# Which half of a block's old keys and queries comes from the chunk that ends last

## The chip, the cores and the metric

The kernel runs on one core of one Trainium2 chip. The metric is the device time of one execution in microseconds (us). The core has five engines with a queue each: TensorE (PE; its weight loads are listed as PEld), VectorE (DVE), ScalarE (ACT), GpSimd (POOL) and SyncE (SP), which here issues DMAs only.

## The reference

Four layers run in turn over 2048 tokens of width 512: attention with a recurrent memory (A), a gated MLP (B), A, B. A's core, cut to what matters:

```python
for s in range(n_seg):                        # 64 segments of 32 tokens
    xs = x[:, s * 32:(s + 1) * 32, :]
    h = concatenate([mem, xs], axis=1)        # 8 memory rows, then 32 tokens
    q, k, v = (einsum('btd,dhe->bhte', h, W) for W in (Wq, Wk, Wv))   # 32 heads of 128
    scores = where(mask, einsum('bhqe,bhke->bhqk', q, k) * scale, -1e9)
    o = einsum('bhqk,bhke->bhqe', softmax(scores), v)
    o = einsum('bhte,hed->btd', o, Wo)
    mem = o[:, :8, :]                         # goes into the next segment
    outs.append(o[:, 8:, :])
```

Each segment needs the memory that the one before it puts out, so the 64 segments of a pass run one after the other.

## The kernel before

There are two passes over A, each 64 segments in 16 blocks of four (128 tokens), and a B layer behind each. One segment takes about 9.7 us.

**New and old rows.** A segment has 40 rows: 8 memory rows and 32 tokens. Only 32 rows fit a column group of TensorE, so the kernel multiplies 32 of them (the memory and the first 24 tokens) by Wq, Wk and Wv inside the segment. The last 8 tokens of a segment depend on no memory. They are called the *old* rows, and are projected ahead, for the four segments of a block at once: four times 8 rows are again 32 (`hB`, copied from the block's transposed input `hT` by GpSimd, L637).

**Chunks.** The projection of `hB` is cut in six chunks of 512 columns, numbered j: 0 and 1 are the queries, 2 and 3 the keys, 4 and 5 the values, the even one for *half 0* of the heads and the odd one for *half 1*. A chunk is 16 matmuls (`b_mms`, L714) into a PSUM bank. ScalarE copies it to `rowsB` (L763), and `b_out` then has it turned, so that heads lie along the free dimension: by a DMA transpose issued by SP (L768), or, for one marked `turned`, by VectorE (L766). The turned queries go to `QTB`, the keys to `KTB`, each with two halves and two buffers, by the block's parity. In the profile they have the names `front` (even blocks) and `old` (odd blocks).

**Where the chunks run.** A segment calls `fill()` three times, at places where TensorE has to wait for the other engines: ahead of `pv(0)`, ahead of the second inverse, and behind `tok_out(0)`. Each call runs the next piece of a generator. For blocks 2, 3 and 4 of the first pass and 1 to 4 of the second it is `b_even`, run over the four segments of the block before. It spreads twelve pieces: one chunk in four quarters into one PSUM bank (`accA`), two whole chunks between them in another (`accB`), and this twice. In the last of the four segments the last two quarters of the second such chunk are run and then its DMA transpose is issued; then comes the last whole chunk, which VectorE turns. Later blocks use `b_units` and are done a segment earlier.

**What a segment needs of them.** `prep_segment(s + 1)` stands at the end of segment s. GpSimd copies the 8 old rows of the segment from `QTB` into columns 32 to 39 of `QQ` (L905, both halves by one instruction of 128x256), and from `KTB` into `KX` (L909, one instruction for each half). `QQ` and `KX` have two buffers each, by the segment's parity. GpSimd's and SP's instructions are put in order by a scheduler; those of TensorE, VectorE and ScalarE stay as written.

**The scores.** `scores(r)` for half r has 16 matmuls of all 40 queries with the new keys `KA` (L975, moving operand `QQ`) and 4 of the queries with the old keys (L979, weights `KX[r]`). TensorE runs: the four projections, the start of the values of half 0, `scores(0)`, the rest of the values of half 0, half of the values of half 1, `scores(1)`. ScalarE takes the exponential (L984), and VectorE multiplies it by the mask into `E` (L987); both inputs are in SBUF. VectorE's order after `scores(0)` is: turn `KA` of half 1 (L952), `E` of half 0, `VA` of half 0 (L1073), `E` of half 1. `pv(0)` (L1024) needs `E` and `VA` of half 0.

Of the kernel before, what the change touches and what calls it, by code (L numbers as in the profile page):

```python
# [16 lines left out]
KT = 4  # L17
# [564 lines left out]
def qk_rhs(w, j, kt, cg):  # L582
    return w[j // 2][:, kt, :].rearrange("p (r gs i eb el) -> p r eb i gs el", r=2, gs=4, i=4, eb=4)[:, j % 2, cg]


def cols_rhs(w, j, kt, cg):
    at = 2048 * (j % 2) + 512 * cg
    return w[j // 2][:, kt, at:at + 512]
# [81 lines left out]
def a_block(tc, c, rows, front, MV_in, RS_in, MV_out, RS_out, ahead, wo, S, first):  # L670
# [6 lines left out]
    with ExitStack() as ctx:  # L677
# [34 lines left out]
        def mm_chunk(ps, lhs, rhs, kts=range(KT)):  # L712

            return [nc.tensor.matmul(ps[32 * cg:32 * cg + 32, :], lhsT=lhs(kt, cg), rhs=rhs(kt, cg), start=(kt == 0), stop=(kt == KT - 1),  # L714
                                     tile_position=(0, 32 * cg)) for kt in kts for cg in range(4)]
# [8 lines left out]
        NKQ = 2  # L724
        KAr = [pers.tile([P, 2, 8, 32, 2], BF16, name=f"KA{i}") for i in range(2)]
        QQr = [pers.tile([P, 2, 8, 40, 2], BF16, name=f"QQ{i}") for i in range(NKQ)]
        KXr = [[pers.tile([P, 4, 32], BF16, name=f"KX{i}{r}") for r in range(2)] for i in range(NKQ)]
        uT = [pers.tile([P, H, 32], BF16, name=f"uT{i}") for i in range(2)]
# [8 lines left out]
        def store_v(bs):  # L737
            nc.sync.dma_start(rows.vb_d[:], bs["VB"].rearrange("p i r e -> p (i r e)"))
# [8 lines left out]
        copies, turns, adds = [], [], []  # L747
# [5 lines left out]
        def b_out(bs, slot, j, ps, turned, stored):  # L753

            if j >= 4:
                nc.scalar.copy(bs["VB"][:, :, j - 4, :], ps.rearrange("p (i e) -> p i e", i=4))
                if turned:
                    ahead.regroup(bs["VB"], bs["VX"], (j - 4,))
                elif stored:
                    store_v(bs)  # L760
                return
            r = rowsB[:, slot, :]
            nc.scalar.copy(r, ps)  # L763
            t = bs[("QTB", "KTB")[j // 2]][:, j % 2]
            if turned:
                turns.append(lambda: nc.vector.transpose(out=t.rearrange("p a b -> p (a b)"), in_=r))  # L766
            else:
                nc.sync.dma_start_transpose(out=t.rearrange("p (i g) k -> p i (g k)", g=4), in_=r.rearrange("t (i e) -> t i e", i=4))  # L768

        def b_mms(bs, j, ps, kts, turned=False):  # L770
            mm_chunk(ps, lambda kt, cg: bs["hB"][:, kt, :],
                     lambda kt, cg: qk_rhs(w, j, kt, cg) if j < 4 and turned else cols_rhs(w, j, kt, cg), kts)
# [23 lines left out]
        def b_even(tb):  # L796

            bs = blk_state[tb]
            for j, others in ((4, (5, 0)), (2, (1, 3))):
                psA = accA.tile([P, 512], F32, name="psb")[:]  # L800
                for kt, other in zip((0, 2), others):
                    b_mms(bs, j, psA, (kt,))
                    yield
                    b_mms(bs, j, psA, (kt + 1,))
                    if kt == 2:
                        copies.append(lambda j=j, psA=psA: b_out(bs, 0, j, psA, False, True))
                    yield
                    psB = accB.tile([P, 512], F32, name="psb")[:]
                    b_mms(bs, other, psB, range(KT), other == 3)
                    copies.insert(0, lambda other=other, psB=psB: b_out(bs, 1, other, psB, other == 3, False))  # L810
                    yield

        def wo_pairs(px, lhs):
# [87 lines left out]
        def prep_segment(s, eng=nc.gpsimd):  # L901
            tb, j4 = s // 4, s % 4
            bs = blk_state[tb]
            QQ = QQr[s % NKQ]
            eng.tensor_copy(QQ[:].rearrange("p r n q two -> p (r n) two q")[:, :, :, 32:40],  # L905
                            bs["QTB"].rearrange("p r (n two) k -> p (r n) two k", two=2)[:, :, :, 8 * j4:8 * j4 + 8])
            KX = KXr[s % NKQ]
            for r in range(2):
                eng.tensor_copy(KX[r][:].rearrange("p g (k i) -> p i g k", i=4),  # L909
                                      bs["KTB"][:, r].rearrange("p (i g) k -> p i g k", i=4)[:, :, :, 8 * j4:8 * j4 + 8])  # L910
            seg_state[s] = dict(QQ=QQ, KX=KX, VX=bs["VX"])

        def fold(px, cross, t1, beside):
# [18 lines left out]
        def segment(s, fill, spare1, spare2, spare3, tail, loads):  # L932
            tb, j4 = s // 4, s % 4
            st = seg_state.pop(s)
            QQ, KX, VX = st["QQ"], st["KX"], st["VX"]
            KA = KAr[s % 2]
# [14 lines left out]
            def qk_T(j, r):  # L951
                nc.vector.transpose(out=(QQ[:, j % 2, :, 0:32] if j < 2 else KA[:, j % 2]).bitcast(F32).rearrange("p n q one -> p n (q one)"), in_=r[:].bitcast(F32))  # L952

# [3 lines left out]
            def ends(q):  # L957

                return q.rearrange("p h (b e) -> p h b e", e=8)[:, :, 0:5:4, :]

            def own(q):

                return q.rearrange("p (i b e) -> p i b e", i=4, b=2)
# [4 lines left out]
            def scores(r):  # L968
# [3 lines left out]
                for i in range(4):  # L972
                    for g in range(4):
                        n = 4 * i + g
                        mms.append(nc.tensor.matmul(pS[32 * g:32 * g + 32, 40 * i:40 * i + 40], lhsT=KA[:, r, n // 2, :, n % 2], rhs=QQ[:, r, n // 2, :, n % 2],  # L975
                                                    start=(i == 0), stop=True, tile_position=(0, 32 * g), skip_group_check=True))
                for g in range(4):
                    q = QQ[:, r].rearrange("p (i g) q two -> p i g two q", i=4)[:, :, g // 2, g % 2, :]
                    mms.append(nc.tensor.matmul(own(pS[32 * g:32 * g + 32, 160:224]), lhsT=KX[r][:, g, :], rhs=ends(q),  # L979
                                                start=False, stop=True, tile_position=(0, 32 * g), skip_group_check=True))  # L980
# [162 lines left out]
            if s + 1 < NSEG:  # L1143
                prep_segment(s + 1)
# [14 lines left out]
        start = nc.vector if first else nc.gpsimd  # L1159
        rows.begin(start)  # L1160
        prep_segment(0, start)
        due, ys = [], []
        seen = pers.tile([P, 1], BF16, name="seen")
# [16 lines left out]
        for s in range(NSEG):  # L1180
            tb, j4 = s // 4, s % 4
# [149 lines left out]
```

## Time and profile before

| | |
|---|---|
| timed runs, median of 3 | 1624.22 us (1623.9 to 1627.45) |
| profiled execution | 1621.89 us |
| its span on the core | 1620.2 us |
| TensorE busy | 1577.7 us, 97% of the span |
| GpSimd busy | 288.2 us, 18% of the span |
| GpSimd's copies into KX (L909) | 254, 0.54 us each in the mean |
| GpSimd's copies into QQ (L905) | 127, 0.49 us each in the mean |
| mean granted clock of TensorE | 0.998 |

The profile is of one execution, on the chip, by the hardware profiler. A row of the timeline has the start in us from the span's start, the duration, the engine, the line, the operation, what it writes and reads with shapes, the number of like instructions merged in the row and, in brackets, the idle time of the engine before it and what ended that. A row of waits has the engine and line that waited, whom for, the total, how many times, and the longest.

### The profile page before, as it was taken

How to read it: one execution, taken by the hardware profiler on the slowest of the kernel's cores; microseconds unless marked ns; L12 is line 12 of the kernel's file. 1: busy time of each engine (PE TensorE's matmuls, PEld its weight loads, DVE VectorE, ACT ScalarE, POOL GpSimd, SP SyncE). 2: the span in 40 equal slices, each digit the busy share in tenths (PEclk: the TensorE clock that was granted, in tenths of full speed). 3: DMA queues.
4: the chain of work that ended last, by engine and by line, in shares of the span. 5: the costliest groups of instructions: out<-in, count | busy, mean ns of one | idle time of the engine just before them, and what ended most of it. 6: DMA issues, size and time to landing. Idle time of an engine off the chain costs nothing.

```text
span 1620.2 us, 91261 instructions
## 1 busy us (share of the span) xinstructions
PE 1577.7 (97%) x41182; PEld 983.8 (61%) x41182; DVE 1070.7 (66%) x3059; ACT 1050.1 (65%) x2281; POOL 288.2 (18%) x604
## 2 busy tenths in 40 slices
PE   5899999999999999999999999999999999999999
PEld 2566666666666666566656656666666666665565
DVE  4576766667776776784366666666677667768622
ACT  3677777777777777660047777777777777776400
POOL 6111111112211221320011111111121112214000
PEclk9999999999999999999999999999999999999999
DMA  9412111113321333277952122121233223425696
GB/s 364 94 42 41 41 44 43 43 43 83 74 56 44 89 83 78 92 184 157 203 161 47 46 42 50 46 47 47 72 87 77 47 69 99 99 52 172 144 197 160
DMA packets 259805, 148.11 MB, mean 91 GB/s; under 512 B 193752, under 2 KB 235840, under 8 KB 259416
## 3 DMA queue, kind: packets, MB, share of 16 engines
q1 hardware_dynamic: 246184, 98.46, 27.8%
q0 software_dynamic: 13232, 43.82, 8.3%
q8 instruction: 322, 5.28, 1.4%
q14 instruction: 67, 0.55, 0.1%
HBM read 59.68 MB, written 37.19 MB: 60 GB/s over the span
## 4 chain that ended last, share of the span: by engine, by line
PE 50%; DMA 4%; DVE 2%; issue 0%; SPq 0%; ACT 0%; POOL 0%; DVEq 0%; ACTq 0%
PE psK L714 6%; PE psQ L714 6%; PE pg L397 5%; PE psb L714 5%; PE pz L296 5%; PE psO L825 4%; PE px L818 3%; PE psV L714 3%; PE psm L714 3%; PE pwB L837 2%; PE psO L1024 2%; PE psT L1016 1%; PE py L440 1%; DMA y_x<-xd 1%; DMA ln_x<-xd 1%; PE psS L975 1%
## 5 line engine op out<-in xcount | busy, mean ns | idle before, releaser
L714 PEld LDWEIGHTS <-hT 128*32 128x32 bf16 x12288 | 343.8, 97 | 265.3 <-DVE hT L924 14.0
L714 PE MATMUL psV<-Wv_sb,hT 128*32 128x512 bf16 x2048 | 165.7, 379 | 0.0
L952 DVE STREAM_TRANSPOSE QQ<-rows 128x256 f32<-128x256 f32 x256 | 113.1, 442 | 77.8 <-ACT rows L949 75.8
L949 ACT CAST rows<-psQ 128x512 bf16<-128x512 f32 x256 | 144.2, 592 | 27.6 <-PE psQ L714 24.9
L984 ACT ACTIVATE S<-psS 128x224 bf16<-128x224 f32 x256 | 92.2, 360 | 100.7 <-PE psS L979 100.5
L1045 DVE TENSOR_TENSOR uT<-psO,Rm 128x128 bf16<-128x128 f32 x256 | 74.7, 292 | 123.0 <-ACT Rm L1042 122.0
L397 PE MATMUL pg<-z,wspT 128*128 128x344 bf16 x1024 | 154.3, 309 | 0.0
L1048 DVE TENSOR_TENSOR uT<-psO,Rt 128x384 bf16<-128x384 f32 x256 | 140.4, 548 | 19.2 <-ACT Rt L1124 17.0
L952 DVE STREAM_TRANSPOSE KA<-rows 128x256 f32<-128x256 f32 x256 | 113.6, 444 | 59.5 <-ACT rows L949 56.4
L714 PE MATMUL psK<-Wv_sb,hT 128*32 128x512 bf16 x2048 | 152.0, 378 | 0.0
L1124 ACT ACTIVATE Rt<-Rt 128x512 f32<-128x512 f32 x256 | 147.3, 622 | 4.0
L825 PE MATMUL psO<-Wo_high,uT 128*32 128x128 bf16 x8192 | 140.2, 219 | 3.8 <-issue 3.7
L714 PE MATMUL psQ<-Wq_sb,hT 128*32 128x512 bf16 x2048 | 136.0, 381 | 7.1 <-DVE xo L448 2.5
L714 PE MATMUL psQ<-Wk_sb,hT 128*32 128x512 bf16 x2048 | 135.3, 380 | 0.0
L714 PE MATMUL psK<-Wk_sb,hT 128*32 128x512 bf16 x2048 | 134.8, 379 | 0.0
L714 PE MATMUL psm<-Wq_sb,hT 128*32 128x512 bf16 x2048 | 134.8, 379 | 0.0
L818 PE MATMUL px<-Wo,uT 128*32 128x256 bf16 x3840 | 133.2, 273 | 0.4
L1121 ACT ACTIVATE Rt<-psT 128x1024 f32<-128x1024 f32 x128 | 131.2, 1025 | 3.2
L397 PEld LDWEIGHTS <-wspT 128*128 128x128 bf16 x1024 | 100.2, 98 | 53.2
L825 PEld LDWEIGHTS <-uT 128*32 128x32 bf16 x8192 | 125.9, 97 | 10.4 <-issue 5.4
L818 PEld LDWEIGHTS <-uT 128*32 128x32 bf16 x4096 | 107.0, 97 | 27.0 <-DVE uT L1045 1.3
L909 POOL COPY KX<-old 128x128 bf16<-128x128 bf16 x128 | 66.0, 535 | 312.1 <-PE psS L979 194.9
(200 smaller groups left out, 2864.7 us busy)
## 6 DMA issues: line engine op xcount, KB each, us to landing
o_d<-o_sb SPq DMA_DIRECT2D x126, 64.0 KB
vb_d<-front SPq DMA_DIRECT2D x30, 256.0 KB
VX<-vb_d SPq DMA_DIRECT2D x120, 64.0 KB
ln_x<-xd SPq DMA_DIRECT2D x26, 256.0 KB
y_o<-o_d POOLq DMA_DIRECT2D x22, 256.0 KB, 3.5
xd<-y_o POOLq DMA_DIRECT2D x22, 256.0 KB, 2.9
Wq_sb<-in_A_Wq_dram POOLq DMA_DIRECT2D x8, 512.0 KB, 8.2
Wk_sb<-in_A_Wk_dram POOLq DMA_DIRECT2D x8, 512.0 KB, 10.0
```

The costliest lines, as they stand in the source:

```text
L296: nc.tensor.matmul(pz[:, c0:c1], lhsT=xnT[:, kt, :], rhs=w_in_sb[:, kt, c0:c1], start=(kt == 0), stop=(kt == KT - 1))
L397: nc.tensor.matmul(pg[t][:, k, 0:344], lhsT=wsp[t][:, st, :], rhs=z(st, 344 * k, 344 * k + 344), start=(st == 0), stop=(st == NT - 1))
L714: return [nc.tensor.matmul(ps[32 * cg:32 * cg + 32, :], lhsT=lhs(kt, cg), rhs=rhs(kt, cg), start=(kt == 0), stop=(kt == KT - 1), tile_posi ...
L818: nc.tensor.matmul(px[at:at + 32, 0:256], lhsT=lhs[:, h, :], rhs=wo_rhs(h, slice(k + 2, None, -2) if h % 2 else slice(k, None, 2)), start= ...
L825: nc.tensor.matmul(pw[32 * cg:32 * cg + 32, :], lhsT=lhs[:, h, :], rhs=wo_rhs(h, cg), start=False, stop=(h == H - 1), tile_position=(0, 32 ...
L949: return r, mms, copy(r[:].rearrange("p (n el two) -> p n el two", n=8, two=2), ps.rearrange("p (n two el) -> p n el two", n=8, two=2))
L952: nc.vector.transpose(out=(QQ[:, j % 2, :, 0:32] if j < 2 else KA[:, j % 2]).bitcast(F32).rearrange("p n q one -> p n (q one)"), in_=r[:]. ...
L984: return nc.scalar.activation(out=S[:, r], in_=psS[:, r, 0:224], func=ACT.Exp, scale=scale)
L1045: nc.vector.tensor_tensor(out=hview(uT_cur[:], r, 24, 32), in0=oview(r, 0, 8), in1=Rm[:, r].rearrange("p g (n q) -> p g n q", q=8), op=ALU ...
L1048: nc.vector.tensor_tensor(out=hview(uT_nxt[:], r, 0, 24), in0=oview(r, 8, 32), in1=rview(r, 0, 24), op=ALU.mult)
L1121: nc.scalar.activation(out=Rt[:], in_=psT[:], func=ACT.Ln)
L1124: nc.scalar.activation(out=rt, in_=rt, func=ACT.Exp, scale=-1.0)
```

## The change

In `b_even` the second quartered chunk is now 3 (half 1's keys), with the whole chunks 2 (half 0's keys) and 1 (half 1's queries) between its quarters. The last whole chunk, the one that VectorE turns, is 1. Before, the quartered one was 2, the whole ones 1 and 3, and VectorE turned 3. In `prep_segment` the copy of the old queries is cut in two instructions, one for each half, and each half's queries stand ahead of its keys. All lines behind move up by one: L975 is L974, L979 is L978 and so on; the copies into QQ are L906 and those into KX L908.

```diff
         def b_even(tb):
...
-            for j, others in ((4, (5, 0)), (2, (1, 3))):
+            for j, others in ((4, (5, 0)), (3, (2, 1))):
...
-                    b_mms(bs, other, psB, range(KT), other == 3)
-                    copies.insert(0, lambda other=other, psB=psB: b_out(bs, 1, other, psB, other == 3, False))
+                    b_mms(bs, other, psB, range(KT), other == 1)
+                    copies.insert(0, lambda other=other, psB=psB: b_out(bs, 1, other, psB, other == 1, False))
...
         def prep_segment(s, eng=nc.gpsimd):
             tb, j4 = s // 4, s % 4
             bs = blk_state[tb]
-            QQ = QQr[s % NKQ]
-            eng.tensor_copy(QQ[:].rearrange("p r n q two -> p (r n) two q")[:, :, :, 32:40],
-                            bs["QTB"].rearrange("p r (n two) k -> p (r n) two k", two=2)[:, :, :, 8 * j4:8 * j4 + 8])
-            KX = KXr[s % NKQ]
+            QQ, KX = QQr[s % NKQ], KXr[s % NKQ]
             for r in range(2):
+                eng.tensor_copy(QQ[:, r].rearrange("p n q two -> p n two q")[:, :, :, 32:40],
+                                bs["QTB"][:, r].rearrange("p (n two) k -> p n two k", two=2)[:, :, :, 8 * j4:8 * j4 + 8])
                 eng.tensor_copy(KX[r][:].rearrange("p g (k i) -> p i g k", i=4),
-                                      bs["KTB"][:, r].rearrange("p (i g) k -> p i g k", i=4)[:, :, :, 8 * j4:8 * j4 + 8])
+                                bs["KTB"][:, r].rearrange("p (i g) k -> p i g k", i=4)[:, :, :, 8 * j4:8 * j4 + 8])
             seg_state[s] = dict(QQ=QQ, KX=KX, VX=bs["VX"])
```

## The prediction, made before the changed kernel was run

> **What bounds the kernel now.** I read the page's busy table first, then the waits of TensorE (weight loads and matmuls), then the timeline at each place where those waits lie.
>
> ```profile
> PE 1577.7 (97%) x41182; PEld 983.8 (61%) x41182; DVE 1070.7 (66%) x3059; ACT 1050.1 (65%) x2281; POOL 288.2 (18%) x604
> ...
> PEclk9999999999999999999999999999999999999999
> ```
>
> TensorE is busy for 97% of the span at the full granted clock, so time can only be won where it stands still. The change touches no matmul's size or number, so only its waits matter. The waits of the weight loads and of the matmuls (engine, line, waited for: us, times, longest):
>
> ```profile
> PEld L975 <- DVE KA L952: 36.6, 144, 1.3
> PEld L979 <- POOL KX L909: 5.3, 5, 1.7
> PE psS L979 <- POOL KX L909: 4.7, 5, 1.6
> ```
>
> The last two rows are one stall, seen on both queues: five times the scores of old keys (L979) wait for GpSimd's copy of them, 4.7 us of matmul time. That is all that GpSimd's copies cost TensorE. The places are the starts of blocks 2, 3, 4 of each pass and of block 1 of the second, the seven blocks fed by `b_even`; two of the seven do not stall. The timeline of one that does (start, duration):
>
> ```profile
> 198.76 1.19 SPq L768 DMA_TRANSPOSE front<-rowsB  x1
> 199.22 0.29 POOL L637 COPY hB<-hT 128x128 bf16<-128x128 bf16 x1 [4.68 <-DMA hT<-ln_xn]
> 200.10 0.70 DVE L766 STREAM_TRANSPOSE front<-rowsB 128x512 bf16<-128x512 bf16 x1
> 202.03 0.28 PE L975 MATMUL psS<-QQ,KA 128*32 128x40 bf16 x16
> 202.66 0.45 DVE L952 STREAM_TRANSPOSE KA<-rows 128x256 f32<-128x256 f32 x1 [0.42 <-ACT rows L949]
> 203.12 1.63 POOL L909 COPY KX<-front 128x128 bf16<-128x128 bf16 x5 [3.61 <-DMA front<-rowsB]
> 203.64 0.10 PEld L979 LDWEIGHTS <-KX 128*32 128x32 bf16 x4 [1.45 <-POOL KX L909]
> 204.55 0.38 PEld L975 LDWEIGHTS <-KA 128*32 128x32 bf16 x16
> ```
>
> The quartered chunk 2 (half 0's old keys) is turned by a DMA issued at 198.76; it lands at about 203.12, when GpSimd starts its copies. Half 0's scores need the first copy and go on at 203.64, 0.52 after it. Half 1's scores begin at 204.55. VectorE turned the other late chunk at 200.10 to 200.80, long before. A boundary without a stall shows the floor for half 1's scores:
>
> ```profile
> 162.86 1.65 POOL L909 COPY KX<-old 128x128 bf16<-128x128 bf16 x5 [2.81 <-DMA old<-rowsB]
> ...
> 163.41 0.12 PEld L979 LDWEIGHTS <-KX 128*32 128x32 bf16 x4
> ...
> 163.96 0.45 DVE L952 STREAM_TRANSPOSE KA<-rows 128x256 f32<-128x256 f32 x1 [0.42 <-ACT rows L949]
> ...
> 164.46 0.25 PEld L975 LDWEIGHTS <-KA 128*32 128x32 bf16 x16 [0.23 <-DVE KA L952]
> ```
>
> They can begin 0.50 after VectorE starts turning half 1's new keys (KA), whatever GpSimd does.
>
> **The change part by part.** Chunks: matmuls, ScalarE copies, DMA turns and VectorE turns keep their number, size and place in each queue; chunks 2, 1, 3 only change slots (one matmul of Wq or of Wk takes 379 ns in either). Cost 0. What moves is who needs the late DMA: now half 0's scores, afterwards half 1's, about 1.1 us later in TensorE's order (203.64 to 204.55 plus the 0.2 of L979 itself). The turns also gain a wait for GpSimd's reads of the same buffer two blocks earlier, long over: 0.
>
> GpSimd's queue: the built program's order at such a boundary is now: queries of segments s and s+1, hB, then (late) keys half 0 of s and s+1, keys half 1 of s and s+1. Afterwards: queries and keys of half 0 for s and s+1, hB, then keys half 1 of s (these wait for the DMA), keys half 1 of s+1, queries half 1 of s, queries half 1 of s+1. So half 0 no longer stalls, but **half 1's scores now wait for the third copy behind the landing**, since their moving operand is QQ. Everything turns on this: the stall is not removed, it is moved and shortened.
>
> Let L be the start of the first late copy. Now, where there is a stall, half 1's scores begin at L+1.42 (204.55-203.12=1.43; the other four give 1.42). Afterwards: five copies take 1.63 to 1.65 with 0.47 for the last, a pitch of 0.29, so the queries' copy starts at L+0.58. Its duration, 128 elements with a stride of two, is in no row: between 0.29 (hB, 128 elements) and 0.48 (the whole 256 elements of QQ); I take 0.40, between them. Then 0.05 until TensorE moves (0.52-0.47). L+1.03. Bounds: 0.58+0.29+0.05=0.92 and 0.58+0.48+0.05=1.11, plus 0.23 if a VectorE mask product runs beside it (a KX copy that took 0.47 alone took 0.70 there): 1.34. The five stalled boundaries by L, KA's start and the present start: 124.11, 124.12, 125.53; 203.12, 202.66, 204.55; 875.43, 875.71, 876.85; 914.62, 915.17, 916.04; 955.14, 954.41, 956.56. The new start is the later of L+1.03 and KA+0.50: gains 0.39, 0.40, 0.39, 0.37, 0.39, together **1.94 us** (0.41 with 1.34, 2.38 with 0.92). The two others (L+1.03 = 163.89 and 995.91 against floors of 164.46 and 996.34) gain and lose nothing. Behind that point TensorE's queue is as before, so the gain stays.
>
> The split copies: one more GpSimd instruction in each of 128 segments. No wait in TensorE's lists but the five names GpSimd in an ordinary segment; the copies there are made for two segments ahead. What they could reach is VectorE. With half 0's queries copied ahead of its keys, GpSimd is busy 0.3 to 0.5 longer just when VectorE forms half 0's mask product E and then VA, which TensorE needs at L1024:
>
> ```profile
> 75.64 0.48 POOL L909 COPY KX<-old 128x128 bf16<-128x128 bf16 x1 [7.39 <-PE psS L979]
> 76.15 0.35 DVE L987 TENSOR_TENSOR E<-S,maskN 128x448 bf16<-128x448 bf16 x1
> 76.42 0.68 DVE L1073 CAST VA<-psK 128x512 bf16<-128x512 f32 x1
> 77.16 0.32 PE L1024 MATMUL psO<-E,VA 64*128 64x80 bf16 x8
> ```
>
> Here VA's end (77.10) is followed by L1024 after 0.06: it is the last to come. That holds in segments 1 to 3 of the first pass alone, which have no fill. Elsewhere the distance is about 0.27 (VA ends 306.74, L1024 at 307.00), so 0.21 us is cover. A single copy beside E lengthens it by 0.04 at most (0.39 at 56.78) or not at all (0.35 at 305.79, with a copy running from 305.52 to 306.00). Cost: 3 x 0.04 = 0.1; bounds 0 and 3 x 0.15 (E took 0.50 beside the train of five). If the cover were gone, see the second rival.
>
> The page "SBUF — State Buffer" of the Trainium skill, section "Who interferes with whom", speaks against the change: a VectorE instruction with two SBUF inputs and a GpSimd instruction that reads SBUF exclude each other, the later one being fully blocked. By it E would wait out the longer pair of copies in every segment. The 0.35 at 305.79 beside a running copy does not show this; the 0.70 of a copy begun just after E agrees with it.
>
> VectorE makes the first segment's copies (29.50 to 30.37); its next work is at 32.21, after 1.84 idle: 0.
>
> Sum: -1.94+0.1 = -1.8. The profiled execution took 1621.89 (span 1620.2 and 1.7 around it) and becomes 1620.1; the median of the timed runs is 2.3 above it, so 1624.2 becomes **1622.4**, 0.11% less. This kernel can be told from no change at about 0.2%, 3.2 us.
>
> **Rivals.** *The stall goes altogether* (faster). If the copies behind the late landing are in time everywhere, the gain is the present starts minus the floors: 0.91+1.39+0.64+0.37+1.65 = 4.96, so 1619.3. It needs earlier landings, not a faster copy. For it: at the two worst boundaries the hT transpose ahead on SP's queue took 2.04 and 2.23 us to issue (195.99 and 947.87) against 1.20 at 869.24, 908.63 and 989.03; with 1.0 less at these two, 0.52+0.25+0.26 of stall would remain, a gain of 3.9 and 1620.3. Against it: nothing in the change shortens that issue.
>
> *GpSimd's pair delays VectorE in every segment* (slower). If E waited for the end of both copies, it would start at 75.64+0.29+0.48 = 76.41 in place of 76.15, 0.26 late; past the cover of 0.21 that is 0.05 in each of some 121 segments, 6.0, and 0.26 in each of three, 0.8: +6.8-1.9 = +4.9, 1629.1. It decides from about 0.25 late on (each 0.01 past the cover is 1.2 us). For it: E took 0.50 for 0.35 beside the train of five (at 204.30). The page named above would lead one to expect it. Against it: even there it lost 0.15, less than the cover.
>
> *The stall only changes place* (no gain: the copies interleave with VectorE's work and L+1.34 holds): 0.4 less, 1623.8. That the change does not do what it says is excluded by the built order, except in this sense.
>
> **How the numbers follow.** The forecast with its bounds, from 2.4 less to no change, and the no-gain case: 0.74, all within 0.2%. Stall gone or nearly: 0.17, faster by over 0.2%. VectorE delayed: 0.09, slower. The range goes from 1619.3, the stall gone, to 1626.0, which takes in a small part of the VectorE case on top of the forecast; the forecast's own range is 1621.8 to 1624.3.
>
> **What would show it.** Right: L979 no longer waits for KX; instead L975's second group waits for QQ at four or five boundaries, L+1.03 after the first late copy, 3.0 us in all; the half copy of QQ takes 0.3 to 0.5; E keeps 0.35 to 0.39 in ordinary segments. Wrong: L975 waits nowhere for GpSimd (first rival), or E starts late in ordinary segments and L1024 follows VA by 0.06 (second), or a new wait on GpSimd inside blocks.

## The result, and the profile after

The changed kernel takes 1626.68 us (median of 16 runs, 1623.23 to 1630.98) beside 1623.94 for the kernel before on the same chip (16 runs, 1620.17 to 1627.45). The ratio is 1.0019, with a 95% interval of 1.001 to 1.0028. In this comparison the change is a loss of about 3 us, where a gain of 1.8 was forecast. The profiled execution took 1626.55 us, with a span of 1624.9.

The busy table and the clock's row of the page after:

```profile
PE 1583.6 (97%) x41159; PEld 975.5 (60%) x41182; DVE 1074.6 (66%) x3060; ACT 1049.1 (65%) x2281; POOL 291.6 (18%) x731
...
PEclk9999999999999999999999999999999999999999
```

TensorE has the same weight loads as before (41182; a few matmul records are missing) and is busy for the same share. GpSimd has 127 instructions more and works 3.4 us longer. VectorE has no more work in the program, and yet it is busy 3.9 us longer: the first sign. The waits of TensorE (who waits for whom: us, times, longest):

```profile
PE psT L1015 <- DVE E L986: 2.1, 3, 1.8
...
PE psS L974 <- POOL QQ L906: 1.4, 3, 0.9
...
PEld L1015 <- DVE E L986: 3.1, 5, 1.9
```

No row names `KX` any more: the stall of 4.7 us is gone, and in its place half 1's scores wait for the late queries, three times, 1.4 us. In the waits alone, then, the change does what it was forecast to do. The boundary that the prediction took as its example, in the timeline after:

```profile
203.06 0.28 PE L974 MATMUL psS<-QQ,KA 128*32 128x40 bf16 x16
...
203.59 0.77 POOL L908 COPY KX<-front 128x128 bf16<-128x128 bf16 x2 [2.79 <-DMA front<-rowsB]
...
204.15 0.95 POOL L906 COPY QQ<-front 128x128 bf16<-128x128 bf16 x3
...
204.66 0.28 PE L974 MATMUL psS<-QQ,KA 128*32 128x40 bf16 x16 [0.20 <-POOL QQ L906]
```

Half 0's scores (203.06) run before the late chunk lands (203.59). Half 1's (204.66) come 1.07 after that copy's start, held by `QQ`. So the boundaries got better, and the time was lost elsewhere. The groups of VectorE's and GpSimd's instructions show where to look (busy us, mean ns of one). Before:

```profile
L987 DVE TENSOR_TENSOR E<-S,maskN 128x448 bf16<-128x448 bf16 x256 | 96.5, 377 | 10.3 <-ACT S L984 4.1
...
L909 POOL COPY KX<-front 128x128 bf16<-128x128 bf16 x126 | 63.6, 537 | 276.8 <-PE psS L979 176.9 <-DMA front<-rowsB 82.1 <-PE psS L998 9.3
```

After:

```profile
L986 DVE TENSOR_TENSOR E<-S,maskN 128x448 bf16<-128x448 bf16 x256 | 101.2, 395 | 7.4 <-ACT S L983 1.9
...
L908 POOL COPY KX<-front 128x128 bf16<-128x128 bf16 x126 | 59.6, 482 | 93.3 <-DMA front<-rowsB 87.6 <-PE psK L714 3.2 <-PE psS L978 2.2
```

The mask products grew by 4.7 us together, and the copies into `KX` shrank by 55 ns each. Neither instruction was edited. The growth is all in the **second** mask product of a segment, that of half 1 (50.8 to 55.9 us in all): 54 of 128 take 0.47 to 0.49 and three take 0.51 or 0.52, where before 123 took 0.39 or 0.40. Half 0's product is unchanged (0.35 in 116 of 128; 115 before). One such segment in the timeline before:

```profile
367.15 0.47 POOL L905 COPY QQ<-front 128x256 bf16<-128x256 bf16 x1 [0.73 <-PE psS L979]
...
367.45 0.39 DVE L987 TENSOR_TENSOR E<-S,maskN 128x448 bf16<-128x448 bf16 x1
367.54 0.63 POOL L909 COPY KX<-front 128x128 bf16<-128x128 bf16 x1
...
367.79 0.10 PEld L1027 LDWEIGHTS <-VX 64*128 64x128 bf16 x2
...
367.89 0.11 PEld L1016 LDWEIGHTS <-ones 64*128 64x128 bf16 x4
```

The same segment after:

```profile
366.39 0.33 POOL L906 COPY QQ<-front 128x128 bf16<-128x128 bf16 x1 [0.49 <-PE psS L978]
...
366.64 0.47 POOL L908 COPY KX<-front 128x128 bf16<-128x128 bf16 x1
366.69 0.48 DVE L986 TENSOR_TENSOR E<-S,maskN 128x448 bf16<-128x448 bf16 x1
...
367.03 0.10 PEld L1026 LDWEIGHTS <-VX 64*128 64x128 bf16 x2
...
367.23 0.11 PEld L1015 LDWEIGHTS <-ones 64*128 64x128 bf16 x4
```

Before, the whole query copy takes 0.47, the copy into `KX` starts 0.09 *after* `E`, and it is the copy that is stretched (0.63); `E` takes 0.39. After, the half query copy takes 0.33, the copy into `KX` starts 0.05 *ahead of* `E`, and it is `E` that is stretched (0.48); the copy takes 0.47. TensorE's token sums (L1016, after L1015: `ones` against `E` of both halves) come next in its queue. Before, their load follows the one ahead at once (367.79+0.10 = 367.89; `E` had ended at 367.84). After, the load ahead ends at 367.13 and the sums' load starts at 367.23, 0.06 behind the end of `E` at 367.17: 0.10 in which nothing is loaded. The row has no bracket of idle time, and in the list of waits the total for L1015 (3.1 us, 2.9 before) is that of five long ones. A delay this short is seen only by laying the same segment of both kernels side by side.

### The profile page after: what moved, and what is told of

It is laid out like the page before. It is cut to its first block, busy times and chain, and to the rows that moved or that the text cites. A ratio compares the mean times of both kernels' runs of the same rounds, so it can differ in the third digit from the quotient of the medians.

```text
span 1624.9 us, 91387 instructions
## 1 busy us (share of the span) xinstructions
PE 1583.6 (97%) x41159; PEld 975.5 (60%) x41182; DVE 1074.6 (66%) x3060; ACT 1049.1 (65%) x2281; POOL 291.6 (18%) x731
## 4 chain that ended last, share of the span: by engine, by line
PE 54%; DVE 2%; DMA 1%; issue 1%; POOL 0%; ACT 0%; DVEq 0%; SPq 0%; POOLq 0%
PE pg L397 9%; PE psQ L714 7%; PE psK L714 7%; PE psb L714 5%; PE psO L825 4%; PE px L818 3%; PE psV L714 3%; PE psm L714 3%; PE pz L296 3%; PE py L440 2%; PE pwB L837 2%; PE psO L1023 2%; PE psT L1015 1%; PE psS L974 1%; DMA xb_d<-ln_xn 1%
## 5 line engine op out<-in xcount | busy, mean ns | idle before, releaser
L714 PEld LDWEIGHTS <-hT 128*32 128x32 bf16 x12288 | 336.3, 97 | 275.1 <-DVE hT L923 12.7
L714 PEld LDWEIGHTS <-hB 128*32 128x32 bf16 x2976 | 76.6, 97 | 54.1 <-issue 22.1
```

## The experiments

**The theory** (theory 1): in the segments whose copies run beside half 1's mask product (the first two of each block, which prepare the last two) the shorter first copy lets the copy of the keys start just ahead of `E`. `E` is then 0.09 longer, and the token sums are that much later. The distance from one segment's first scores to the next one's bears this out: in the median it is 0.09 longer than before in the first and the second segment of a block, and unchanged in the other two. With 54 products of that length, 50 of them in these places, that is 54 x 0.09 = 4.9 us lost.

**Its rivals**: the loss comes from the swap of chunks; or it comes from GpSimd's larger number of instructions, whatever their order; or it is chance, since single runs of one kernel differ by several us. The cuts of code below are against the changed kernel.

### The split without the swap

The kernel before with the change's edit of `prep_segment`; `b_even` as before.

```diff
-            for j, others in ((4, (5, 0)), (3, (2, 1))):
+            for j, others in ((4, (5, 0)), (2, (1, 3))):
...
```

> Only prep_segment of the change: half 1's queries copied on their own, keys of half 1 right behind them; the chunks as in the kernel before. Theory 1 (in segments 0 and 1 of a block, GpSimd's copy of half 1's old keys now starts just ahead of VectorE's second mask product E, which takes 0.48 in place of 0.39, and TensorE's token sums wait for it): E's second product 0.48 in about 62 segments, 62 x 0.09 = +5.6 us over the kernel before, about 1629.5, and the five stalls of L979's matmuls on KX (5 us) as before. Theory 2 (the split costs nothing; what the changed kernel lost lies in the B layer and at the start of the second pass, 1.4 and 1.5 us in its one profile, by chance or by the new order of the first copies there): within 1 us of the kernel before.

Measured: 1628.09 us (6 runs), ratio 1.0037 (1.0024 to 1.005), which is 6.0 us more than before. The mask products:

```profile
L986 DVE TENSOR_TENSOR E<-S,maskN 128x448 bf16<-128x448 bf16 x256 | 101.1, 395 | 8.9 <-ACT S L983 2.6
```

The split alone brings the 395 ns and the loss, without the gain at the boundaries. Half 1's `E` takes 0.47 to 0.49 in 47 segments, where 62 were expected, and 0.41 or 0.42 in 18 more. Leaving out the boundaries, the segments are 0.09 longer in the median in the first and second place of a block, and not longer in the others.

### The swap without the split

`prep_segment` as before, `b_even` as changed.

```diff
-                eng.tensor_copy(QQ[:, r]..., bs["QTB"][:, r]...)      # each half ahead of its keys
+            eng.tensor_copy(QQ[:]..., bs["QTB"]...)                   # both halves at once, first
```

> Only b_even's new order of chunks; one copy for the queries of both halves, as before. In the built order that copy now stands behind the late keys of half 1 at the seven boundaries, so half 0's scores wait for it, from their first matmul on: until L+1.10 by the rows of before (two keys' copies 0.58, one of 0.47, 0.05). With the starts of half 0's scores in the profile of before (123.27, 163.11, 201.81, 874.86, 914.32, 953.56, 994.99) the stalls are 1.94, 0.85, 2.41, 1.67, 1.40, 2.68, 0.99 = 11.9 in place of 5.0: +7.0, about 1631. Both theories expect this; E's second product 0.39 by both. A result near the kernel before would say that the boundaries were read wrongly.

Measured: 1627.58 us (5 runs), ratio 1.004 (1.0028 to 1.0052). `E` keeps 0.39 (123 of 128). The ratio is worth 6.5 us, where 7.0 were expected. The loss is at the boundaries, where half 0's scores now need a copy that reads both halves' queries, one half of them from the late chunk. The same boundary in this kernel's timeline:

```profile
204.18 0.75 POOL L909 COPY KX<-front 128x128 bf16<-128x128 bf16 x2 [3.57 <-DMA front<-rowsB]
204.74 0.87 POOL L905 COPY QQ<-front 128x256 bf16<-128x256 bf16 x2
205.27 0.28 PE L975 MATMUL psS<-QQ,KA 128*32 128x40 bf16 x16 [2.00 <-POOL QQ L905]
```

So the two edits belong together: the swap needs halves at the boundaries. It does not need them inside a block.

### The split where the swap needs it

The change, but with the query copy whole for the last two segments of each block. These are the ones whose copies ran beside half 1's `E`. The first two segments, prepared at the boundary, keep the halves.

```diff
+            whole = j4 > 1
+            if whole:
+                eng.tensor_copy(QQ[:]..., bs["QTB"]...)
             for r in range(2):
-                eng.tensor_copy(QQ[:, r]..., bs["QTB"][:, r]...)
+                if not whole:
+                    eng.tensor_copy(QQ[:, r]..., bs["QTB"][:, r]...)
```

> The whole change, but the queries' copy is split only for segments 0 and 1 of a block, whose copies do not run beside E's second product; for segments 2 and 3 it is one instruction again. Theory 1: E's second product back at 0.39, the gain of the boundaries alone is left: in the profiles of before and of the change it is 0.62+1.16+0.70+0.47+0.71 = 3.7, so about 1620.3, faster than both. Theory 2: as the changed kernel, about 1626 to 1627.

Measured: 1620.03 us (12 runs), ratio 0.9986 (0.9972 to 0.9999). A group and a stretch of the timeline:

```profile
L991 DVE TENSOR_TENSOR E<-S,maskN 128x448 bf16<-128x448 bf16 x256 | 96.4, 376 | 8.2 <-ACT S L988 2.5
```

```profile
364.82 0.47 POOL L907 COPY QQ<-front 128x256 bf16<-128x256 bf16 x1 [0.73 <-PE psS L983]
...
365.11 0.39 DVE L991 TENSOR_TENSOR E<-S,maskN 128x448 bf16<-128x448 bf16 x1
365.20 0.64 POOL L913 COPY KX<-front 128x128 bf16<-128x128 bf16 x1
```

`E` leads again by 0.09 and takes 0.39. In the median no place of a block is longer than before, and the boundaries keep the change's gain. This version is the fastest of the kernels here, though its interval ends only just below 1.

### As many instructions, but the longer copy first

Whether the number of GpSimd's instructions counts is told by a kernel that has all of the change's and more work. For the last two segments of a block the second query copy reads both halves (that of half 0 is repeated), so that it takes as long as before the change, and the number of instructions stays that of the change.

```diff
+                if r and j4 > 1:
+                    eng.tensor_copy(QQ[:]..., bs["QTB"]...)
+                else:
-                eng.tensor_copy(QQ[:, r]..., bs["QTB"][:, r]...)
+                    eng.tensor_copy(QQ[:, r]..., bs["QTB"][:, r]...)
```

> The whole change, but for segments 2 and 3 of a block the second of the two query copies copies both halves (256 elements, half 0's queries a second time), so GpSimd has as many instructions as in the change and more to do, and the copy of half 1's keys behind it starts about 0.14 later, just behind the start of E's second product and not just ahead of it. Theory 1, in the form that the earlier start wins: E's second product 0.39, the keys' copy beside it 0.6 to 0.7, time as with the split for the first segments only, about 1620.3. Rival 3 (more GpSimd instructions or more of its work slow VectorE, whichever starts first): E's second product 0.48 or more, time as the changed kernel or slower, 1626 to 1630. Theory 2: 1626 to 1627.

Measured: 1622.82 us (12 runs), ratio 1.0004 (0.9992 to 1.0016).

```profile
364.42 0.47 POOL L907 COPY QQ<-front 128x256 bf16<-128x256 bf16 x1 [0.50 <-PE psS L982]
...
364.71 0.39 DVE L990 TENSOR_TENSOR E<-S,maskN 128x448 bf16<-128x448 bf16 x1
364.80 0.64 POOL L912 COPY KX<-front 128x128 bf16<-128x128 bf16 x1
```

More work on GpSimd, and `E` is back at 0.39 and the segments at their length of before: the rival of the number of instructions falls. What decides is the 0.09 by which one start leads the other. About 1620.3 was expected, and this kernel's time is 2.8 us above that of the split-where-needed. Why isn't settled: its profile has 1.0 us of TensorE's wait at L296 of the B layer (0 to 1.3 over the profiles of all kernels) and the window of half clock told of below, and neither belongs to its edit.

### A short copy put between, which missed its aim

A copy of 16 elements was to delay the keys' copy by its own length.

```diff
+                if r and j4 > 1:
+                    eng.tensor_copy(QQ[:, r]...[:, 0:1, :, 32:40], bs["QTB"][:, r]...[:, 0:1, ...])
                 eng.tensor_copy(KX[r]..., bs["KTB"][:, r]...)
```

> The whole change, with one more small GpSimd copy (16 elements of half 1's queries a second time) between half 1's queries and its keys in segments 2 and 3 of a block. The keys' copy then starts 0.1 to 0.2 later, behind the start of E's second product. Theory 1: E's second product 0.39, the keys' copy beside it 0.6 to 0.7, TensorE's token sums on time: 3 to 5 us less than the changed kernel in the same call, and 1 to 3 less than the kernel before, although GpSimd has one instruction more. Rival 3 (more GpSimd instructions slow VectorE): as the changed kernel or slower. This also tells whether the 1622.8 of the long second copy was that kernel's own or chance.

Measured: 1623.91 us (12 runs), ratio 0.9999 (0.9988 to 1.001).

```profile
365.48 0.33 POOL L906 COPY QQ<-front 128x128 bf16<-128x128 bf16 x1 [0.49 <-PE psS L981]
...
365.72 0.47 POOL L911 COPY KX<-front 128x128 bf16<-128x128 bf16 x1
365.77 0.48 DVE L989 TENSOR_TENSOR E<-S,maskN 128x448 bf16<-128x448 bf16 x1
...
365.99 0.33 POOL L909 COPY QQ<-front 128x16 bf16<-128x16 bf16 x1
```

The scheduler put the short copy *behind* the keys' copy, so no gap was made, and nothing follows from its time for or against the rival. It gives a second point for the size of the effect instead. In the first segments of a block the keys' copy leads `E` by 0.05, and `E` takes 0.48; in the second ones it leads by 0.12, and `E` takes 0.415. One of the second:

```profile
375.77 0.47 POOL L911 COPY KX<-front 128x128 bf16<-128x128 bf16 x1
...
375.89 0.41 DVE L989 TENSOR_TENSOR E<-S,maskN 128x448 bf16<-128x448 bf16 x1
```

Lead and loss add up to 0.14 in both places (0.05 and 0.09, 0.12 and 0.023): `E` ends as late as if it had stood still until 0.14 behind the copy's start. The profiles of all kernels agree: at every lead from 0.01 to 0.14 (278 products of half 1 beside one copy into `KX`) the sum is 0.14 or 0.15, and from 0.15 on (95 products) `E` takes 0.39. The segments follow: in the median the first ones are 0.09 longer than before, the second ones 0.02.

### The same kernels again

The two kernels and the best version were run once more together on another chip.

> The changed kernel once more, for a second profile and a ratio beside the next three. Theory 1: E's second product 0.48 in about 60 segments, +5.3; the seven boundaries 3 to 4 less; +1.5 to +2.5 over the kernel before, and the rest of what the first profile showed (a window of half the granted clock at the start of the second pass, 1.5 us, and a wait for xb_d in the B layer, 1.4) comes and goes by chance. Theory 2: the half-clock window and the xb_d wait are there again at the same places, and without them the time would be that of the kernel before.

> The kernel before once more, for a second profile. Theory 1: E's second product 0.39 in every ordinary segment, the stalls of L979's matmuls on KX some 3 to 7 us in all, by where the late DMA lands; a half-clock window at the start of the second pass may come here too. Theory 2: no half-clock window and no xb_d wait, as in the first profile.

> The split for the first two segments of a block alone, once more, to bound its gain: 1 to 3.5 us less than the kernel before, 3 to 5 less than the change. If the first result was chance: no different from the kernel before.

Measured: the change 1624.44 us (12 runs), ratio 1.0006 (0.9996 to 1.0017); the kernel before 1622.59 (8 runs), 0.9992 (0.9976 to 1.0007) against the pool of 35 runs of itself; the split where it is needed 1621.97 (12 runs), 0.9983 (0.997 to 0.9995). In the profiles half 1's `E` takes 0.47 to 0.49 in 58 segments of the change, and 0.39 in both others. The order of the three kernels stays. The interval of the change now takes in 1, so this comparison alone doesn't tell it from the kernel before; the size of the loss against before is 0.06% here and 0.19% in the first comparison, and the intervals of the two overlap only between 1.001 and 1.0017.

### Is the window of half clock the change's doing?

The first profile of the change has 3.4 us at half the granted clock at the start of the second pass, after some 2.9 us in which TensorE waits; the first 32 weight loads take 2.73 us there, and 1.45 in the first profile of the kernel before. The first two profiles of the kernel before had no such window, and seven of the eight of changed kernels had it (all but the first of the split where it is needed). So the kernel before was profiled three times more, unchanged.

> The kernel before, unchanged, profiled a third time. Question: is the 3.4 us window of half granted clock at the start of the second pass (some 1.5 us of time, present in the profiles of the change, absent in the two of the kernel before) a thing of chance, or does the change bring it? If chance: one or more of these three profiles of the kernel before have it (the other kernels had it in 7 of 8 profiles). If the change brings it: none has. In either case the second mask product takes 0.39 in all ordinary segments.

> As for the third profile of the kernel before: with the window if it comes by chance, without if the change brings it.

> As for the third profile of the kernel before: with the window if it comes by chance, without if the change brings it.

Measured, one run each: 1619.25, 1626.22 and 1627.23 us. The last two have the window. Stretches of the third of them (us, busy time and instructions of each engine, granted clock, DMA share, GB/s):

```profile
830.00:833.30 3.30, 1.03 (x5) 0.29 (x3) 3.23 (x7) 1.25 (x4) 1.80 (x6) 1.00 0.98 351
833.30:836.70 3.40, 3.19 (x32) 1.42 (x36) 1.39 (x4) 1.08 (x3) 0.48 (x2) 0.50 0.48 178
836.70:840.00 3.30, 3.30 (x89) 1.74 (x85) 1.53 (x4) 2.02 (x4) 0.48 (x1) 1.00 0.02 5
```

With the window the second stretch holds 32 matmul records at a clock of 0.50. So it comes to the kernel before too: two of five against seven of eight. It isn't made by the change, and whether the change makes it more frequent can't be told from so few. What it costs is seen in the kernel before: from the first scores of the first pass's last segment to those of the second pass's first segment it takes 159.4 us in the mean of the two profiles with the window and 157.9 in the three without, 1.5 more. If the difference in frequency were real, it would be worth about 0.7 us of the loss. In all five profiles of the kernel before half 1's `E` takes 0.39, in 119 to 122 of 128 segments.

## Why the prediction was wrong

**The bound** (right): TensorE at 97% and full clock; only its waits could change.

**The boundaries** (right in mechanism, too small in size): half 0 no longer stalls, and half 1's scores begin at L+1.04, L+1.07 and L+0.95 where they wait at all (125.42 to 126.46, 203.59 to 204.66, 960.16 to 961.11) against L+1.03 forecast; the half copy of `QQ` takes 0.33, and up to 0.46 beside a mask product, against 0.40 taken. Half 1's scores wait for `QQ` at three boundaries, 1.4 us in all (two or three and 1.1 to 2.3 over the six profiles of kernels with both swap and halves), where four or five and 3.0 were forecast. The mis-sized term is the present start, L+1.42. That is the start of the *weight loads* (204.55), which run ahead. It was compared with a start of matmuls, and the first matmul of half 1 came at 204.76, L+1.64:

```profile
204.55 0.38 PEld L975 LDWEIGHTS <-KA 128*32 128x32 bf16 x16
...
204.76 0.27 PE L975 MATMUL psS<-QQ,KA 128*32 128x40 bf16 x16
```

So a stalled boundary gains 1.64-1.04 = 0.60, not 0.39: 2.9 us over the five (0.51 at the one that KA's turn then bounds). Measured over all seven boundaries, from the first scores of the segment before to half 1's scores, these six profiles are 3.9 us below the five of the kernel before in the mean; up to the next segment's first scores 3.5 of it are left. A single boundary of one kernel differs by up to 1.5 us from profile to profile. What goes beyond 2.9 is not assigned.

**The split copies** (the step that failed): the prediction asked only what a longer GpSimd pair does to half 0's `E` and `VA`, ahead of L1024, and found cover of 0.21. There nothing happened: that `E` stays at 0.35. It did not look at half 1's `E`, and that one has no cover. The token sums' load starts 0.05 behind its end before the change (367.84 and 367.89), which looks like room; but it starts 0.06 behind it after the change as well (367.17 and 367.23), where no load had run for 0.10, and the median is 0.05 in both kernels. So all that is added to this `E` is lost: 0.09 here, and in the kernel with the short copy 0.02 for 0.023. The prediction also asked how long GpSimd is busy, not which instruction starts first. The row that would have told was in the trace of before: a copy into `KX` of 0.62 to 0.64 starting 0.09 or 0.10 after `E` in 43 of the 64 first and second segments, and of 0.69 or 0.70 starting 0.02 or 0.03 after it in 16 more. A copy stretched by 0.16 says that the two collide there, and that the loser is the later one; a first copy shorter by 0.14 moves the start past the other. At 0.1 for the whole kernel, the term was put at a fiftieth of the 4.9 that it is.

**The second rival** (right pair of engines and right sign, wrong place): it had VectorE delayed in every segment by GpSimd's pair and a time of 1629.1, but at half 0's `E`, in all segments, and decided by a delay past 0.21. The chance of 0.09 rested on the cover at that place. **The first rival** (the stall goes altogether) did not come: three waits remain at the boundaries. **The third** did not come either: `QQ` beside a mask product took 0.42 and 0.46, and L+1.34 was nowhere reached.

**The rule on who is blocked.** The page "SBUF — State Buffer" of the Trainium skill, section "Who interferes with whom", says that the order of issue decides who blocks, and this case agrees: copy 0.09 behind, the copy stretched by 0.16; copy 0.05 ahead, `E` stretched by 0.09. The same page of the Trainium skill, section "Summary: rules for kernel authors", says that in such a pair the second one to issue fully blocks until the first finishes. By that `E` would have ended at 367.50 (the copy's end, 367.11, and 0.39) and not at 367.17; here the measurement differs, and `E` loses only what is left of 0.14 us from the copy's start. The prediction weighed the rule at half 0 and set it aside on the 0.35 at 305.79, where the copy had started 0.27 ahead. That row was right; it was a case of one lead, taken for all.

**The sum**: 4.9 lost and 2.9 to 3.9 gained makes 1.0 to 2.0 us slower. The measured ratios are worth 0.19% (1.6 to 4.5 us by the interval) and 0.06% (from 0.6 less to 2.8 more). The second interval holds all of it, the first only what lies above 1.6; beyond that the size isn't settled.

## What to carry to other kernels

When an edit moves an instruction of GpSimd by a tenth of a microsecond, list the VectorE instructions with two SBUF inputs that it then starts ahead of or behind, and follow the one that loses to its reader; a copy that is longer than its like in the profile of before marks the place. Split a copy only where someone waits for its half. Compare a matmul's start with a matmul's start: weight loads run ahead of it.

## What the runs showed of the hardware

- A copy of GpSimd (128x128) and a mask product of VectorE (128x448, both inputs in SBUF) collide by their starts: copy 0.09 later, copy 0.63 and product 0.39; copy 0.05 earlier, 0.47 and 0.48; copy 0.12 earlier, product 0.415; copy 0.15 or more earlier, product 0.39 again (95 of them). For half 1's product, loss and lead add up to 0.14 or 0.15 at every lead from 0.01 to 0.14 (278 products of 13 profiles).
- The GpSimd copies of 16 elements per partition took 0.31 in the mean (64 of them, each right behind a copy of the keys), nearly as long as one of 128 of the same kind (0.33); one of 256 took 0.47.
- A window of half granted clock, 3.4 us long, follows a wait of TensorE of 2.9 us in some executions of the same kernel and not in others; with it the kernel before takes 1.5 us more between the passes.
